# A chunked state-space scan followed by hash-routed experts on one Trainium2 core: scan scalings and routing arithmetic on GpSimd, halved masked copies, and other orders of gathers, weight sums and products

## The chip, the cores and the metric

The kernel runs on one core of a Trainium2 chip. The metric is the device time of one execution in microseconds (us). Lower is better. TensorE, VectorE, ScalarE and GpSimd have instruction queues of their own, in the profile PE, DVE, ACT and POOL; SyncE (SP) issues most transfers, ScalarE some, and GpSimd all the indirect ones (gathers and scatters by a list of row numbers).

## The reference

Two computations follow each other. The first is a scan over 768 tokens for 4 batches of 8 heads (head width 32, state width 16), in chunks: within a chunk a causal product, across chunks a state that decays.

```python
cum = np.cumsum(la, axis=-1)                      # la = log(clip(a)), per chunk
L = np.exp(cum[:, :, :, None] - cum[:, :, None, :]) * causal
M = np.einsum('bhin,bhjn->bhij', Cc, Bc) * L
y[:, :, sl] = np.einsum('bhij,bhjd->bhid', M, xc) \
            + np.einsum('bhin,bhnd->bhid', Cc, state) * np.exp(cum)[:, :, :, None]
state = decay_full * state + sum_over_j(Bc * decay_from_j * xc)
```

The second takes the 3072 rows of 256 numbers that come out, sends each to one of 8 experts by its token's id, and applies that expert's two layers (256 to 1024 to 256, all float32):

```python
expert_idx = token_ids * np.int64(2654435761) % np.int64(E)
for e in range(E):
    mask = expert_idx == e
    out[mask] = np.maximum(x[mask] @ w1[e], 0.0) @ w2[e]
```

## The kernel before, in words

The order on each engine is the order of the code: nothing reorders it. Each engine works its queue off in order, so an instruction that waits holds all those behind it on that engine.

**The scan** works in six pieces of 128 tokens of all four batches (`k` = 0 to 5), with time units of 64. B and C are loaded in four larger pieces of 1, 1, 2 and 2 (`PIECES`, `load_rows`). `factors` gives each row its decay factors, `scale_rows` multiplies the loaded rows by them (512 or 1024 columns, always on VectorE, L234), `turn_rows` transposes them in 32 by 32 blocks (VectorE, L241), and `mask_c` makes two copies of C with every other head zero (ScalarE). `gram(k)` is the product of B and C, 64 small products into four PSUM banks (L523). `masked(k)` copies its lower triangle into a block whose other half stays zero (`copy_predicated`, 2048 columns, L528), `intra(k)` multiplies that with x (L572), `dstates(k)` and `states(k)` make the states (L551, L555 on VectorE), and `inter(k)` adds C times the state (L583). `y_evict` and `y_store` bring the piece to DRAM. In the loop (L664 to L693) piece k's `states`, then some work of `piece(k)`, `intra` and `inter` come first, then `gram`, `masked` and `dstates` of piece k + 1.

**The routing** is spread over `piece(k)` and the loop's end: the experts' ids as a mask (`rt_ids`, `rt_mask`, L289 to L302), counts (`rt_count`), places, halves and overflow of each expert (`rt_prefix`, `rt_place`, L316 to L359, in piece 2), the slot of each token (`rt_rank`, L366 to L369, on GpSimd; `rt_slot_a` to `rt_slot_d`, L373 to L400, in piece 3), one-hot rows (`rt_lanes`: twelve on GpSimd, L411, and twelve on VectorE, L407; `rt_tiles`), products that turn them into a table (`rt_table`) and the index lists (`to_index`, L432 to L453). The first five gathers (`gather`, L480) follow.

**The experts** (place 0 is the one with the most tokens) do both layers with seven products instead of eight per 2 by 2 block (Strassen's scheme in Winograd's form). So there are sums on weights (`sums_w1`, L711 to L714; `sums_w2`, L720 to L723), on tokens (`sums_x`) and on hidden rows (`sums_h`), all on VectorE. `step(p)` runs expert p's first layer (`up`, L770) beside expert p - 1's second (`down`, L812), in seven slots: sums, two `up` products, a tile of gathered tokens turned for the next expert (`turn_x`, L488), a finished tile turned and scattered (`put`, L838 to L847), one `down`. The four sums of `sums_w1` stand in slot 0, the four of `sums_w2` in slot 1, and `ask(1)` asks for one more gather in every slot from the third on. A gather needs one of eight buffers (`gpool`), a scatter one of four (`o_sb`). Steps 0 to 7 are followed by step 8, which has only the last second layer; then four tiles are put out (L948 to L950). A loop over overflow tiles (L958) runs as often as a count says, here not at all.

The chain of small sums before a product's result:

```python
        elif what == 7:                                    # up(), L787
            dve.tensor_tensor(out=u3, in0=src, in1=st["p1"], op=OP.add)
            z = ps[:, st["z"], 0:2 * n].rearrange("q (i n) -> q i n", i=2)
            dve.tensor_tensor(out=hq(2), in0=z, in1=u3, op=OP.add)
            act.activation(hq(2), hq(2), AF.Relu)
```

## Time and profile before

| what | value |
|---|---|
| time, median of three runs | 287.68 us (284.52 to 287.95) |
| the profiled execution | 285.23 us |
| its span | 283.4 us |
| TensorE busy | 224.9 us (79%), 2577 products |
| weight loads on TensorE | 205.7 us (73%) |
| VectorE busy | 201.5 us (71%) |
| ScalarE busy | 76.3 us (27%) |
| GpSimd busy | 79.0 us (28%) |
| mean granted TensorE clock | 0.92 of full speed |

The span is one execution seen by the hardware profiler. Busy shares are means over stages: to 86 us the scan, from there to about 270 the experts, then the end. Products on TensorE are pipelined and their ends modelled, so a busy TensorE is not one at its peak. "[0.9 <-DVE x L1]" behind a row says how long the engine was idle before it and which instruction ended that; "issue" is idle time for which the profile shows no wait. A granted clock of 1.0 is 2.4 GHz, 0.5 is 1.2 GHz.

### The profile page before, as it was taken

To read this page: it belongs to the slowest core of one execution; us is meant where nothing else is said; L and a number is where in the kernel's file an instruction comes from. 1 tells how busy PE (TensorE), PEld (TensorE's weight loads), DVE (VectorE), ACT (ScalarE), POOL (GpSimd) and SP (SyncE) were. 2 spreads that over 40 slices of the span, in tenths; PEclk is the share of its full clock that TensorE was granted. 3 is DMA by queue.
4 is the path that set the end of the run, shared out by engine and by line. 5 is a ranking of instruction groups with operands and counts; after the bars stand their busy time and mean duration, and the time that the engine had idled before them with its cause. 6 is when DMAs were issued, how large, how long until landed. Compare 5 with 4: busy or idle time off the path is not lost. (4 is left out here: it accounts for less than half of the span.)

```text
span 283.4 us, 6377 instructions
## 1 busy us (share of the span) xinstructions
PE 224.9 (79%) x2577; PEld 205.7 (73%) x2579; DVE 201.5 (71%) x393; ACT 76.3 (27%) x177; POOL 79.0 (28%) x113
## 2 busy tenths in 40 slices
PE   7885775576579768798799989499989999999820
PEld 2773654465469758788689989399979999998810
DVE  7879768999808529977977958836876886776310
ACT  4314152043116512210312223221242242313010
POOL 8800003019443760001121501710132130312250
PEclk9689799579958997999999999989999999999995
DMA  5899998507958334015316305610901500500110
GB/s 127 135 173 141 173 178 176 192 22 207 294 173 245 97 106 148 19 21 191 123 57 208 126 2 185 203 38 5 312 20 58 166 26 13 172 33 6 51 59 1
DMA packets 51890, 33.19 MB, mean 117 GB/s; under 512 B 30714, under 2 KB 46194, under 8 KB 51860
## 3 DMA queue, kind: packets, MB, share of 16 engines
q1 hardware_dynamic: 47444, 24.41, 34.4%
q0 software_dynamic: 2400, 6.43, 7.0%
q10 hardware_dynamic: 2016, 1.93, 2.3%
q8 instruction: 21, 0.34, 0.6%
q14 instruction: 9, 0.07, 0.1%
HBM read 26.47 MB, written 6.42 MB: 116 GB/s over the span
## 5 line engine op out<-in xcount | busy, mean ns | idle before, releaser
L847 POOL DMA_INDIRECT out_dram<-o_sb,idx_out x25 | 27.9, 1117 | 73.7 <-ACT o_sb L843 58.9
L480 POOL DMA_INDIRECT xg<-y_tokens,idx_in x25 | 27.5, 1098 | 75.3 <-PE ps L838 46.6
L770 PE MATMUL ps<-t,s 128*128 128x202 f32 (+7 forms) x192 | 37.6, 333 | 2.2 <-DVE t L730 1.6
L770 PEld LDWEIGHTS ps<-t,s 128*128 128x128 f32 x192 | 32.8, 194 | 3.2 <-ACT xT L494 1.8
L812 PE MATMUL ps<-t,s 128*128 128x202 f32 (+7 forms) x192 | 34.9, 326 | 0.0
L812 PEld LDWEIGHTS ps<-t,s 128*128 128x128 f32 x192 | 31.3, 190 | 0.0
L770 PE MATMUL ps<-xT,w 128*128 128x202 f32 (+7 forms) x128 | 26.2, 342 | 0.0
L792 ACT ACTIVATE hx<-hx 128x404 f32<-128x404 f32 (+7 forms) x16 | 8.4, 525 | 57.6 <-DVE hx L791 57.6
L770 PEld LDWEIGHTS ps<-xT,w 128*128 128x128 f32 x128 | 22.6, 200 | 0.8 <-ACT p1e L777 0.7
L572 PE MATMUL ps<-x,w 128*64 128x64 f32 x384 | 15.6, 251 | 7.1 <-issue 2.6
L572 PEld LDWEIGHTS ps<-x,w 128*64 128x64 f32 x384 | 14.7, 164 | 8.3 <-issue 4.5
L770 PE MATMUL ps<-t,w 128*128 128x202 f32 (+7 forms) x64 | 14.5, 351 | 7.1 <-DVE u L789 5.6
L528 DVE COPY_PREDICATED w<-cmask,ps 128x2048 f32<-128x2048 int32 x6 | 15.2, 2532 | 4.9 <-PE ps L523 4.9
L770 PEld LDWEIGHTS ps<-t,w 128*128 128x128 f32 x64 | 11.0, 198 | 9.1 <-DVE u L789 7.3
L838 PE MATMUL ps<-ident,xT 128*128 128x128 f32 x50 | 9.8, 281 | 6.7 <-ACT o_sb L843 6.1
L812 PE MATMUL ps<-hx,s 128*128 128x202 f32 (+7 forms) x64 | 12.1, 331 | 2.5 <-DVE xT L830 2.5
L770 PE MATMUL ps<-xT,s 128*128 128x202 f32 (+7 forms) x64 | 13.8, 344 | 0.0
L843 ACT ACTIVATE o_sb<-ps 128x256 f32<-128x256 f32 x23 | 8.7, 380 | 18.6 <-PE ps L838 12.2
L411 POOL TENSOR_SCALAR laneoh<-iota,lane 128x128 bf16<-128x128 f32 x12 | 9.0, 765 | 16.6 <-DVE stile L400 16.6
L494 ACT ACTIVATE xT<-ps 128x256 f32<-128x256 f32 x23 | 8.6, 377 | 16.6 <-PE ps L488 14.7
L523 PE MATMUL ps<-ce,bt 32*64 32x128 f32 x384 | 8.9, 315 | 5.1 <-ACT ce L251 2.8
L812 PEld LDWEIGHTS ps<-hx,s 128*128 128x128 f32 x64 | 10.5, 189 | 3.4 <-DVE xT L830 3.4
(189 smaller groups left out, 442.1 us busy)
## 6 DMA issues: line engine op xcount, KB each, us to landing
w<-in_moe_w_dram SPq DMA_DIRECT2D x8, 1024.0 KB, 6.4
w<-in_moe_w_dram SPq DMA_DIRECT2D x13, 512.0 KB, 4.8
x<-in_x_dram SPq DMA_DIRECT2D x12, 256.0 KB, 6.4
y_tokens<-y_sb SPq DMA_DIRECT2D x6, 512.0 KB, 3.4
w<-in_moe_w_dram ACTq DMA_DIRECT2D x3, 512.0 KB
raw<-in_B_dram SPq DMA_DIRECT2D x8, 128.0 KB, 6.0
raw<-in_C_dram SPq DMA_DIRECT2D x8, 128.0 KB, 4.7
raw<-in_B_dram SPq DMA_DIRECT2D x8, 64.0 KB, 2.1
```

Source lines behind the costliest of these rows:

```text
L411: eng.tensor_scalar(out=laneoh[:, i], in0=iota_n, scalar1=lane[:, i:i + 1], scalar2=None, op0=OP.is_equal)
L480: pool_e.indirect_dma_start(out=xg[k], out_offset=None, in_=y_dram[0:n, :], in_offset=bass.IndirectOffsetOnAxis(ap=idx_in[:, k:k + 1], axi ...
L494: act.activation(o, i, AF.Copy)
L523: pe.matmul(out=ps[u * T:(u + 1) * T, BM + b, g * P:(g + 1) * P].rearrange("q (e i) -> q e i", e=2), lhsT=bts[k][r, g, c], rhs=ces[k][r, g ...
L528: dve.copy_predicated(out=m_sb, mask=cmask.bitcast(I32).rearrange("q j i -> q (j i)").unsqueeze(1).to_broadcast([P, NB, 2 * G * T]), data= ...
L572: pe.matmul(out=o[:, 0], lhsT=m_sb[:, b, h * T:(h + 1) * T], rhs=xs[k][:, b * H + h], start=first, stop=True, skip_group_check=True)
L770: pe.matmul(out=ps[:, bank, i * n:(i + 1) * n], lhsT=lhs[:, (q0 + i) * P:(q0 + i + 1) * P], rhs=rhs, start=(first and i == 0), stop=True, ...
L792: act.activation(hq(2), hq(2), AF.Relu)
L812: pe.matmul(out=ps[:, bank, 0:n], lhsT=lhs(q), rhs=rhs(q), start=(first and q == 0), stop=True, skip_group_check=True)
L838: pe.transpose(out=ps[:, bank, i * P:(i + 1) * P], in_=xT[:, i, k * P:(k + 1) * P], identity=ident)
L843: act.activation(o_sb, ps[:, bank, 0:DM], AF.Copy)
L847: st = pool_e.indirect_dma_start(out=out[:], out_offset=bass.IndirectOffsetOnAxis(ap=idx, axis=0), in_=o_sb, in_offset=None, bounds_check= ...
```

## The change

In the scan, five of the eight scalings (`scale_rows` for C of piece 1 and for all of load pieces 2 and 3) go to GpSimd, as do the small sums for the unit decays (`rg`), the mask of the ids, and the routing's arithmetic on shifts, overflow and slots, partly with other operations of the same value (a comparison is a subtraction and a test of the sign). `gram`, `masked` and `intra` work in two halves of two batches each, so that the products of a half can begin when its half of the masked copy is done. The ids are turned before the loop, the loads are issued in another order (ids and x of piece 0 ahead of piece 1's rows), GpSimd clears the last two x buffers after its first scaling, and the table's products stand ahead of piece 5's `gram`. The eight decays by head go to ScalarE.

In the experts, a gather is asked for whenever a tile has been turned, the sums on weights are dealt out one to a slot (`sums_w2` from the fourth slot on), the `up` products of steps 1 and 2 and the `down` products of all steps have another order, and the last expert's second half begins at a multiple of 128 slots. The last `down` is done in two column parts of 128 and 56, each put out at once, after the two tiles that are complete before; a drain stands on GpSimd behind the tiles of the expert before it.

```diff
+        if pj == order[-1]:
+            at = -(-at // P) * P
...
     load_rows(0, 0, sp4)
     load_rows(0, 1, [act] * NB)
+    sp_e.dma_start(out=tok, in_=tok_h.bitcast(I32).rearrange("(c p two) -> c p two", c=NCH, two=2))
+    load_x(0)
     load_rows(1, 0, sp4)
     load_rows(1, 1, sp4)
-    load_x(0)
-    load_x(1)
-    sp_e.dma_start(out=tok, in_=tok_h.bitcast(I32).rearrange("(c p two) -> c p two", c=NCH, two=2))
...
+    def rt_shift():
+        pool_e.tensor_tensor(out=ovt, in0=tend, in1=ovt, op=OP.subtract)
...
+    def rt_slots():
         g2 = small("g2", sh)
+        eng = pool_e
+        for g, from_, far in ((g1, half, sel[:, 2]), (g2, half2, ovt)):
+            eng.tensor_tensor(out=g, in0=val, in1=ex(from_), op=OP.subtract)
+            eng.tensor_scalar(out=g, in0=g, scalar1=0.0, scalar2=None, op0=OP.is_ge)
+            eng.tensor_tensor(out=g, in0=g, in1=ex(far), op=OP.mult)
...
+    def masked(k, bs):
+        b0, b1 = bs[0], bs[-1] + 1
         dve.copy_predicated(
+            out=m_sb[:, b0:b1],
+            mask=cmask.bitcast(I32).rearrange("q j i -> q (j i)").unsqueeze(1).to_broadcast([P, len(bs), 2 * G * T]),
+            data=ps[:, BM + b0:BM + b1])
+
+    LO, HI = range(0, NB // 2), range(NB // 2, NB)
...
     def piece(k):
         if k == 0:
-            scale_rows(dve, 2, 0)
             turn_rows(2, 0)
         elif k == 1:
-            scale_rows(dve, 2, 1)
             turn_rows(2, 1)
             mask_c(2, (act, act))
+            state["who"] = rt_prefix()
+            scale_rows(pool_e, 3, 0)
+        elif k == 2:
+            rt_place(state["who"])
+            rt_shift()
+            load_regs()
+            turn_rows(3, 0)
             mask_c(3, (act, act))
-            rt_mask()
-        elif k == 2:
-            state["n"], state["poh"] = rt_prefix()
-            rt_place(state["n"], state["poh"])
-            load_regs()
-            scale_rows(dve, 3, 0)
-            turn_rows(3, 0)
-            rt_rank(pool_e)
+            scale_rows(pool_e, 3, 1)
+            rt_slots()
         elif k == 3:
-            scale_rows(dve, 3, 1)
             turn_rows(3, 1)
             mask_c(4, (act, act))
...
+        if k == 4:
+            rt_table(BB, 0)
         if k + 1 < NPR:
-            gram(k + 1)
-            masked(k + 1)
+            gram(k + 1, LO)
+            masked(k + 1, LO)
+            gram(k + 1, HI)
+            masked(k + 1, HI)
             dstates(k + 1)
...
+    UPS = [(0, 6, 1), (0, 5, 2), (0, 7, 1), (2, 6, 0), (0, 4, 1), (0, 3, 2), (2, 7, 0), (2, 5, 2), (2, 4, 0), (2, 3, 2)]
+    DOWN = [1, 2, 6, 7, 5, 4, 3]
...
                 turn_x(k)
                 turned.add(k)
+                ask(1)
...
             if s == 0 and 0 < p < E - 1:
-                sums_w1(p + 1, dve)
-            if s == 1 and 0 < p < E:
-                sums_w2(p, dve)
-            if s >= 2:
-                ask(1)
+                sums.append(sums_w1(p + 1))
+            if s == 3 and p > 0:
+                sums.append(sums_w2(p))
+            for x in sums:
+                next(x, None)
...
+    for s, w in enumerate([1, 2, 6, 7, 4, 5]):
+        if s < 4:
+            sums_h(E - 1, s)
+        down(E - 1, w, 3 + BK[w], dst)
+        if puts:
+            put(puts.pop(0), BQ)
+            if not puts:
+                pool_e.drain()
+    assert not puts
+    mid = [k for k in outs if done_at[k] == E - 1 and k * P < base[E - 1, 1]]
+    for i, k in enumerate(mid):
+        put(k, (BQ, BT)[i % 2], (act, dve)[i % 2])
+    down(E - 1, 3, 3 + BK[3], dst, PARTS)
```

What this does to the queues, at three places. First GpSimd from its tables to the routing; x_99 and x_100 are the last two x buffers. Before:

```order
L176 IOTA iota_165 128x8
L176 IOTA iota_167 128x8
L176 IOTA iota_169 128x128
L176 IOTA iota_171 128x24
L176 IOTA iota_173 128x1
L188 MEMSET ctab 128x1 x24
L192 MEMSET x_99 64x32x32 x2
L192 MEMSET x_100 64x32x32 x2
L366 TENSOR_TENSOR val<-pin,cnt 128x192
L367 TENSOR_TENSOR val<-val,cnt 128x192
L368 TENSOR_SCALAR val<-val 128x192
L369 TENSOR_TENSOR val<-val,shift 128x8x8
```

and now, from the mask on, where `rows` are scaled rows:

```order
L314 TENSOR_SCALAR mask_266<-eid 128x24 x8
L240 TENSOR_TENSOR rows_397<-raw_119,fac_244 128x512
L625 MEMSET x_99 64x32x32 x2
L625 MEMSET x_100 64x32x32 x2
L240 TENSOR_TENSOR rows_489<-raw_475,fac_310 128x1024
L240 TENSOR_TENSOR rows_491<-raw_482,fac_310 128x1024
L347 TENSOR_TENSOR shift<-sel,pin 128x8
L348 TENSOR_SCALAR shift<-shift 128x8
L349 TENSOR_SCALAR half_289<-sel 128x8
L350 TENSOR_TENSOR ov<-pin,shift 128x8
L351 TENSOR_TENSOR ov<-ov,half_289 128x8
L353 TENSOR_TENSOR who<-poh,iota_190 128x64
```

Three scalings and the mask stand there now, the clearing of the x buffers lies behind the first of them, and the routing's small steps follow.

Second, GpSimd from its one-hot rows (laneoh) to the last scatter; xg is a gathered tile, out_dram the output. Before:

```order
L411 TENSOR_SCALAR laneoh<-iota_169,lane 128x128 x12
L480 DMA xg<-y_tokens,idx_in 128x256 x23
L847 DMA out_dram<-o_sb,idx_out 3072x256
L480 DMA xg<-y_tokens,idx_in 128x256 x2
L847 DMA out_dram<-o_sb,idx_out 3072x256 x24
```

and now:

```order
L412 TENSOR_SCALAR laneoh<-iota_194,lanes 128x128 x12
L481 DMA xg<-y_tokens,idx_in 128x256 x19
L863 DMA out_dram<-o_sb,idx_out 3072x256
L481 DMA xg<-y_tokens,idx_in 128x256 x3
L863 DMA out_dram<-o_sb,idx_out 3072x256
L481 DMA xg<-y_tokens,idx_in 128x256
L863 DMA out_dram<-o_sb,idx_out 3072x256
L481 DMA xg<-y_tokens,idx_in 128x256
L863 DMA out_dram<-o_sb,idx_out 3072x256 x2
L481 DMA xg<-y_tokens,idx_in 128x256
L863 DMA out_dram<-o_sb,idx_out 3072x256 x20
```

Before, 23 gathers stood ahead of the first scatter; now 19 do, and the last six gathers alternate with scatters.

Third, VectorE in piece 3, from the scaling of C's last rows to the slots' sum (slot_f). Before:

```order
L234 TENSOR_TENSOR rows_970<-raw_480,fac_334 128x1024
L241 STREAM_TRANSPOSE ct<-rows_970 128x4x8x32
L373 TENSOR_TENSOR g_268<-val,sel 128x192
L374 TENSOR_TENSOR g_268<-g_268,sel 128x192
L376 TENSOR_SCALAR half_982<-sel 128x8
L381 TENSOR_TENSOR g_984<-val,half_982 128x192
L382 TENSOR_TENSOR g_984<-g_984,ovt 128x192
L383 TENSOR_TENSOR val<-val,sel 128x192
L384 TENSOR_TENSOR g_268<-g_268,g_984 128x192
L387 TENSOR_TENSOR val<-val,g_268 128x192
L388 TENSOR_TENSOR val<-val,mask_264 128x192
L393 TENSOR_REDUCE slot_f<-val 128x24
```

and now, from the masked copy before it to the one behind it (lanes is the same sum):

```order
L524 COPY_PREDICATED w_131<-cmask,ps 128x1024 x2
L550 TENSOR_TENSOR zd<-d_sb,z 128x256
L554 TENSOR_TENSOR z<-zd,ge_sb 128x256
L550 TENSOR_TENSOR zd<-d_sb,z 128x256
L554 TENSOR_TENSOR z<-zd,ge_sb 128x256
L247 STREAM_TRANSPOSE ct<-rows_837 128x4x8x32
L395 TENSOR_REDUCE lanes<-val 128x24
L396 CAST slot_i<-lanes 128x24
L398 TENSOR_SCALAR part<-slot_i 128x24
L399 TENSOR_SCALAR part<-slot_i 128x24
L401 CAST lanes<-part 128x48
L524 COPY_PREDICATED w_131<-cmask,ps 128x1024 x2
```

The scaling and eight slot instructions are gone from VectorE, and the slots' sum, ahead of the masked copy, reads what GpSimd writes.

## Rows read from the trace of the kernel before

**Rows 1.** Stretches (us): busy time and instructions per engine, PEclk, DMA share, GB/s

```profile
core 0: us, PE busy (x) PEld busy (x) DVE busy (x) ACT busy (x) POOL busy (x), PEclk, DMA share, GB/s
...
110.13:131.42 21.29, 18.18 (x100) 17.22 (x100) 17.45 (x32) 3.50 (x8) 1.02 (x1) 0.96 0.29 96
131.42:152.18 20.76, 17.86 (x106) 16.86 (x106) 16.84 (x31) 4.12 (x10) 3.94 (x3) 1.00 0.37 119
152.18:173.51 21.33, 20.58 (x128) 19.77 (x127) 16.56 (x31) 6.43 (x17) 4.81 (x4) 1.00 0.26 82
173.51:198.85 25.34, 21.33 (x124) 20.75 (x124) 16.66 (x31) 5.95 (x15) 8.05 (x7) 0.93 0.36 118
198.85:220.47 21.62, 20.31 (x129) 19.45 (x129) 16.39 (x31) 6.74 (x18) 5.20 (x5) 1.00 0.36 125
220.47:239.98 19.51, 19.51 (x126) 18.91 (x125) 16.20 (x31) 5.94 (x16) 3.38 (x3) 1.00 0.24 75
```

**Rows 2.** Order of time, VectorE in the scan: start us, us, engine, line, operation

```profile
25.61 2.52 DVE L528 COPY_PREDICATED w<-cmask,ps 128x2048 f32<-128x2048 int32 x1
...
30.92 1.22 DVE L234 TENSOR_TENSOR rows<-raw,fac 128x1024 f32<-128x1024 f32 x1
...
32.17 2.02 DVE L241 STREAM_TRANSPOSE ct<-rows 128x1024 f32<-128x1024 f32 x1
...
36.91 2.52 DVE L528 COPY_PREDICATED w<-cmask,ps 128x2048 f32<-128x2048 int32 x1 [2.54 <-PE ps L523]
...
41.78 0.55 DVE L316 TENSOR_TENSOR_SCAN pin<-rstc,cnt 128x192 f32<-128x192 f32 x1
...
48.09 0.17 DVE L359 TENSOR_TENSOR ovt<-ovt,sel 128x8 f32<-128x8 f32 x1
...
51.40 2.53 DVE L528 COPY_PREDICATED w<-cmask,ps 128x2048 f32<-128x2048 int32 x1
...
58.68 0.34 DVE L373 TENSOR_TENSOR g<-val,sel 128x192 f32<-128x192 f32 x1
...
61.24 0.36 DVE L388 TENSOR_TENSOR val<-val,mask 128x192 f32<-128x192 f32 x1
...
62.88 2.53 DVE L528 COPY_PREDICATED w<-cmask,ps 128x2048 f32<-128x2048 int32 x1
...
75.20 0.17 DVE L435 TENSOR_SCALAR idx_in<-tva 128x25 int32<-128x25 f32 x1
```

**Rows 3.** Order of time in the scan, SyncE's x loads and GpSimd

```profile
7.79 6.27 SPq L124 DMA_DIRECT2D x<-in_x_dram  x4
...
9.54 4.12 POOL L192 MEMSET x<- 64x1024 f32 x4
...
42.49 0.59 POOL L366 TENSOR_TENSOR val<-pin,cnt 128x192 f32<-128x192 f32 x1 [28.83 <-DVE pin L316]
...
46.05 0.29 POOL L369 TENSOR_TENSOR val<-val,shift 128x64 f32<-128x64 f32 x1 [1.44 <-DVE shift L345]
```

**Rows 4.** Single lines: count, duration in ns (min/median/max), first and last start

```profile
L411 POOL TENSOR_SCALAR laneoh<-iota,lane x12: 592/610/1403, 63.0 to 71.4; 128x128 bf16<-128x128 f32 x12
...
L555 DVE TENSOR_TENSOR z<-zd,ge_sb x10: 424/425/544, 22.1 to 77.6; 128x256 f32<-128x256 f32 x10
```

**Rows 5.** TensorE's waits from 28 to 86 us: total us, times, longest

```profile
PE ps L572 <- issue: 2.6, 1, 2.6
```

**Rows 6.** Order of time in the experts: a scatter, ScalarE's and TensorE's wait

```profile
158.90 1.37 POOL L847 DMA_INDIRECT out_dram<-o_sb,idx_out  x1 [0.30 <-issue]
...
181.78 0.38 ACT L843 ACTIVATE o_sb<-ps 128x256 f32<-128x256 f32 x1 [6.18 <-DMA out_dram<-o_sb,idx_out]
...
182.22 0.44 PE L838 MATMUL ps<-ident,xT 128*128 128x128 f32 x2 [4.01 <-ACT o_sb L843]
```

**Rows 7.** The end: GpSimd's last scatter, and the closing line's drains (ns)

```profile
275.40 0.98 POOL L847 DMA_INDIRECT out_dram<-o_sb,idx_out  x1 [0.30 <-issue]
...
L1030 POOLq DRAIN  x3: 45/103/4155, 278.4 to 283.2; - x3
```

More of the change, by code (lines that the diff above doesn't have):

```diff
@@ L312 @@
     dve.memset(rstc[:, :, 0:1], 0.0)
+    ones_e = route.tile([P, E], F32)
+    dve.memset(ones_e, 1.0)
+    half = sel[:, 0]
+    nn = pin[:, :, NCH - 1]
     def rt_prefix():
@@ L398, in rt_slot_d @@
                           op0=OP.logical_shift_right)
-        dve.tensor_copy(out=lane, in_=part[:, 0])
-        dve.tensor_copy(out=stile, in_=part[:, 1])
+        dve.tensor_copy(out=lanes, in_=part)
     CG = 6
@@ L514, in decays_by_heads, with gram @@
         for e in range(2):
-            dve.tensor_scalar(out=ge_sb[:, :, :, e], in0=g_sb, scalar1=par[:, e:e + 1], scalar2=None, op0=OP.mult)
-    def gram(k):
+            act.activation(ge_sb[:, :, :, e], g_sb, AF.Copy, scale=par[:, e:e + 1])
+    def gram(k, bs):
         for g in range(G):
             for u in range(2):
-                for b in range(NB):
+                for b in bs:
                     r = slice(32 * b, 32 * b + 32)
@@ L568, in intra @@
     def intra(k):
-        for h in range(H):
-            for b in range(NB):
-                o, first = y_out(b, h, 1)
-                pe.matmul(out=o[:, 0], lhsT=m_sb[:, b, h * T:(h + 1) * T], rhs=xs[k][:, b * H + h],
-                          start=first, stop=True, skip_group_check=True)
+        for bs in (LO, HI):
+            for h in range(H):
+                for b in bs:
+                    o, first = y_out(b, h, 1)
+                    pe.matmul(out=o[:, 0], lhsT=m_sb[:, b, h * T:(h + 1) * T], rhs=xs[k][:, b * H + h],
+                              start=first, stop=True, skip_group_check=True)
     def inter(k):
@@ L799, in up, with down @@
             act.activation(hq(1), hq(1), AF.Relu)
-    def down(p, what, bank, st):
+        if what in (5, 7) and "z" in st and "u3" in st:
+            dve.tensor_tensor(out=hq(2), in0=st["z"], in1=st["u3"], op=OP.add)
+            act.activation(hq(2), hq(2), AF.Relu)
+    def down(p, what, bank, st, parts=()):
         n = HALF[p]
@@ L810, in down @@
         first = what in (1, 6, 5)
+        if parts:
+            for i, (c0, c1) in enumerate(parts):
+                for q in range(Q4):
+                    pe.matmul(out=ps[:, bank, c0:c1], lhsT=lhs(q), rhs=rhs(q)[:, c0:c1], start=False, stop=True,
+                              skip_group_check=True)
+                dve.tensor_tensor(out=xT[:, 0, slots(p, 1)][:, c0:c1], in0=ps[:, bank, c0:c1], in1=st["u2"][:, c0:c1],
+                                  op=OP.add)
+                put(slots(p, 1).start // P + i, (BQ, BT)[i], (act, dve)[i], c1 - c0)
+            return
         for q in range(Q4):
@@ L902, in step @@
             else:
-                ups = [(q0, w, BK[w]) for q0 in (0, 2) for w in (UP_E if p < NEAR - 1 else UP)]
+                ups = UPS if p < NEAR - 1 else [(q0, w, BK[w]) for q0 in (0, 2) for w in UP]
+        ups = list(ups)
+        sums = []
         downs = list(DOWN) if p > 0 else []
@@ L944, in step @@
             load_w2(p + 1)
-    for p in range(E + 1):
+    for p in range(E):
         step(p)
-    last = [k for k in outs if done_at[k] == E - 1]
-    for i, k in enumerate(last):
-        put(k, (BQ, BT, 0, 1)[i % 4], (act, dve)[i % 2])
+    dst = {}
+    puts = [k for k in outs if done_at[k] == E - 2]
+    for s, w in enumerate([1, 2, 6, 7, 4, 5]):
[11 more added lines that the diff above has]
+    down(E - 1, 3, 3 + BK[3], dst, PARTS)
     _, rn = nc.values_load_multi_w_load_instructions(
```

242 lines of the change are left out of this document (113 added, 129 removed).

## The prediction

> **What bounds the kernel now.** I read the table of stretches first, then the order of time inside the scan and inside the experts, then who waits for whom, then the end. A piece is 128 tokens of each of the four batches; the scan has six, k = 0 to 5, and the experts run in nine steps, 0 to 8. Four things are to be seen.
>
> The scan's loop hangs on VectorE's own order. Per piece it runs the state sums, a scaling (1.22 us), a transposition (2.02) and the masked copy (2.52 for 2048 columns), and TensorE's products of the piece start only when the whole masked copy is over [rows 2]. Between the masked copies of pieces 2 and 3 stands the whole routing, 41.78 to 48.26 us; between those of 3 and 4 stand nine slot instructions, 58.68 to 61.60 [rows 2]. The copies of pieces 1 to 4 end at 28.1, 39.4, 53.9 and 65.4 [rows 2].
>
> The expert steps take 19.5 us where nothing is in the way: step 6, TensorE busy all the time [rows 1]. Steps 1 and 2 take 21.3 and 20.8 with TensorE busy 18.2 and 17.9, step 3 21.3 with 20.6, step 4 25.3, step 5 21.6 with 20.3 [rows 1].
>
> Step 4's excess is one stall: ScalarE waits 6.18 us for an earlier scatter's buffer, TensorE 4.01 us for ScalarE [rows 6]. The first scatter started at 158.90, right behind a gather, since GpSimd's queue held all but two of the gathers ahead of it [rows 6]. The step's granted clock is 0.93, and TensorE's busy time is 1.8 us above step 6's [rows 1].
>
> At the end four scatters follow one another on GpSimd after the last product, 0.98 us each and 0.30 between, the last from 275.40 on, and a drain of 4.16 us on GpSimd's queue closes the program [rows 7].
>
> **The scan, part by part.** The sum is made against the profiled execution: 285.2 us, 283.4 of them span; the median of the three runs is 287.7, the lowest 284.5.
>
> *Scalings on GpSimd.* Five of eight move there. The trace has none on that engine. A product of two inputs took 0.59 us for 192 columns and 0.29 for 64 [rows 3], so 2.3 ns a column and 0.15 fixed: 1.3 us for 512 columns, 2.5 for 1024. The lower end is the 1.22 that VectorE takes; upward I allow twice the value, 5.0, because the scaling reads three strides at once and the rows don't. I take 2.5.
>
> *Start.* Half copies let piece 0's products begin when half is copied, and the small sums of decays leave VectorE. But GpSimd first clears two x buffers (4.12 us [rows 3]), now behind the scaling of piece 1, and only then scales for piece 2. VectorE's order puts that transposition ahead of piece 1's masked copy, so it now waits for GpSimd. The loads of piece 1's rows are issued behind the ids and two x loads, which at 1.6 us an issue [rows 3] puts their landing, an estimate, at 13 to 14; 13.7 + 1.3 + 4.1 + 2.5 = 21.6, say 22, where VectorE could come at 20. Masked copy 1 then ends at 22 + 2.0 + 2.5 = 26.5: 1.5 gained.
>
> *Pieces 1 to 2.* The scaling (1.2) and the mask leave; the first seven routing instructions come in (about 2.7 of the 6.5, an estimate by their share), but they lie in VectorE's idle time of 2.54 before masked copy 2 [rows 2]; the product on the ids that held TensorE is made before the loop. Copy 2 ends near 36: 2 more gained.
>
> *Pieces 2 to 3.* Of 6.5 us of routing seven instructions stay, like the last at 0.17 or little more [rows 2], 1.3; 2.7 have moved forward, the rest is GpSimd's. The scaling goes: 14.5 - 5.2 - 1.2 = 8.1 between the ends of the copies. ScalarE's load of the experts' numbers now stands ahead of the mask of this piece's C, which I charge with 0.5. Copy 3 ends near 44.5: 9.4 gained in all.
>
> *Pieces 3 to 4.* Scaling and eight slot instructions leave VectorE (4.1). In their place GpSimd does the scaling (2.5) and ten slot instructions of 0.59 and more [rows 3], 6.6 with their waits, after the scaling before and the shift: from about 41 to 51. VectorE is ready for the slots' sum at 48 and waits 3. Masked copy 4 is queued behind that sum. It ends at 55, against 65.4: 10.2 gained.
>
> *Piece 4 to the gathers.* The table's products now stand ahead of piece 5's on TensorE and wait for GpSimd's twelve one-hot rows; VectorE's masked copy 5 follows, and the index only then. The token index, written at 75.20 [rows 2], comes near 66.4: 8.8 gained. The first gathers follow as before.
>
> *What comes to light.* TensorE has gaps that the profile calls issue, up to 2.6 us [rows 5], at places where VectorE was mostly the later one. With VectorE faster I charge 2. Scan: **-6.8**.
>
> One rule speaks against all this. VectorE's two-input sums and GpSimd's reading instructions did meet: the one-hot row on GpSimd took 0.61 in the middle and 1.40 at most, the state product 0.43 in the middle and 0.54 at most [rows 4]. The Trainium skill, SBUF — State Buffer, section "Who interferes with whom", says that a VectorE instruction with two SBUF inputs and a GpSimd instruction that reads SBUF exclude each other, the second one blocked until the first has finished. GpSimd's 1.40 agrees with it in size, VectorE's 0.54 does not: it was delayed by 0.1, not by a whole row of 0.6. So I leave the states at their price; the other reading is a rival below.
>
> **The experts.** Steps 1 and 2: the products come in an order where none reads what VectorE has just been handed, and the sums on weights are dealt out one per slot instead of four in a row. VectorE's 17 us and TensorE's 18 remain, so I put the steps at 18.5 and 18.3: 5.3 gained (at least 2, if VectorE's lag stays; at most 6). Step 3 falls to its busy 20.6 (0.7) and step 5 to its 20.3 (1.3), as the sums no longer come in lumps of four. Step 4: a gather is asked for when a buffer is freed, so the scatters stand between the gathers and none waits for buffers of later tiles; 4.0 of stall and 1.5 of slow clock go, 5.5. Sum 12.8; for a new wait somewhere I take 0.8 off: **-12** (bounds -8 and -14).
>
> **The end.** The last product is done in two column parts of 128 and 56, each followed by its own scatter, and two of the four tiles go out before it. GpSimd's scatters stay 1.28 apart, so the chain begins at about 269 and its last starts near 273: **-2.5**. A drain on GpSimd is added after step 6's tiles are out, where GpSimd has some 4 us to spare. What the closing drain then takes no row shows: 0.05 us where nothing was issued before it, 4.16 after fifty indirect transfers [rows 7]. Four stand behind the new one, so I go by the row nearer to that: 0.5, **-3.6**; at the other end 0.
>
> 285.2 - 6.8 - 12 - 2.5 - 3.6 = 260.3; with half the distance to the median of the runs, 261.5.
>
> **The rivals.** *GpSimd becomes the scan's bound.* At 5.0 us a scaling, three of the four long ones stand on the path: 7.5 more, the scan gains nothing, 268 to 269. For it: the wait at piece 3 is there already at 2.5. Against: by rows 3 a product costs 0.15 us and 2.3 ns a column, not 5.
>
> *VectorE is blocked.* If each of four groups of state sums waits for a running scaling to end, up to 2.5 each, the scan loses 10 and ends 3 behind: 271. That is the page's rule taken in full. Against it stands the 0.54 of rows 4.
>
> *The stall of step 4 stays*, because the new scatter order still meets slow transfers: 5.5 less, 267.
>
> *Nearly no change:* both of the first two with the experts' lower bound: 285.2 + 3 + 3 - 8 - 2.5 = 280.7.
>
> *Slower:* the same chain on GpSimd, if scalings with three strides cost over 10 us each. Four scalings at 7.5 more are 30, which uses up the gain of 25 and ends near 290. It decides from 9 us on. Nothing in rows 3 comes near.
>
> **How the numbers follow.** Forecast 0.62, GpSimd as the bound 0.17, blocked VectorE 0.06, the stall stays 0.06, nearly no change 0.06, slower 0.03. A measurement of this kernel tells 2% (5.8 us) from no change. Faster by more than that: 0.62 + 0.17 + 0.06 + 0.06 = 0.91; within it 0.06; slower 0.03. The range starts at the best of all terms, 285.2 - 11 - 14 - 7 = 253 (the scan's 11 with scalings as short as VectorE's), with 2 for the runs' spread below, 251, and ends where the two middle rivals with the runs' spread (2.4) end, 274.
>
> **What would show it.** Right: masked copies ending near 26, 36, 44 and 55; VectorE idle for about 3 us before the slots' sum, with GpSimd named; steps 1 and 2 near 18.5 and step 4 near 20; no wait of ScalarE for a scatter; a closing drain under 1 us. Wrong: scalings on GpSimd far from 2.5, transpositions that wait for GpSimd in every piece, the first gather later than 70, or a closing drain still at 4.

## The result, and the profile after

| | before | after |
|---|---|---|
| median of four runs | 286.10 us (282.06 to 287.95) | 257.75 us (257.01 to 258.11) |
| ratio, 95% interval | | 0.9087 [0.9024, 0.9149] |
| profiled execution, its span | 285.23, 283.4 | 257.79, 256.1 |
| TensorE, VectorE, GpSimd busy | 79%, 71%, 28% | 87%, 74%, 38% |

Medians here and below are over all runs of a kernel, ratios over its fast runs alone; the profiled executions of scan_only, experts_only and no_drain lie 1.5 to 1.9% above their kernels' fastest run. By the medians 28.4 us were gained; the forecast's sum was 24.9. The page of after, busy time by engine, the clock in 40 slices, and the chain that ended last:

```profile
PE 223.3 (87%) x2584; PEld 206.1 (80%) x2584; DVE 188.9 (74%) x362; ACT 77.2 (30%) x180; POOL 97.6 (38%) x152
...
PEclk9658997698595799999999999999999999999995
...
PE 58%; DVE 14%; DMA 12%; issue 6%; POOL 4%; ACT 3%; ACTq 0%; POOLq 0%
```

From the 15th slice to the last but one the granted clock stands at nine tenths or more: from step 1 to step 6 TensorE no longer stops. The stretches of steps 1 to 6, each from a step's first product to that of the next, answer to [rows 1]:

```profile
core 0: us, PE busy (x) PEld busy (x) DVE busy (x) ACT busy (x) POOL busy (x), PEclk, DMA share, GB/s
103.53:120.58 17.05, 17.02 (x98) 16.53 (x99) 16.26 (x32) 4.22 (x9) 1.00 (x1) 1.00 0.40 131
120.58:137.72 17.14, 17.14 (x105) 16.89 (x105) 16.04 (x32) 3.99 (x10) 4.93 (x4) 1.00 0.49 152
137.72:158.08 20.36, 20.28 (x127) 19.89 (x127) 16.73 (x32) 6.42 (x17) 8.49 (x7) 1.00 0.32 105
158.08:177.67 19.59, 19.48 (x124) 19.13 (x124) 16.10 (x31) 5.87 (x15) 3.57 (x3) 1.00 0.39 126
177.67:197.74 20.07, 19.95 (x130) 19.56 (x130) 16.00 (x31) 6.76 (x18) 5.23 (x5) 1.00 0.46 152
197.74:217.19 19.45, 19.32 (x126) 18.98 (x126) 15.92 (x31) 6.07 (x16) 3.27 (x3) 1.00 0.22 73
```

TensorE is busy for all but 0.1 us of each step. Steps 1 and 2 went from 21.29 and 20.76 to 17.05 and 17.14, step 4 from 25.34 to 19.59.

The order of time in the scan, GpSimd first, then VectorE; this answers to [rows 2]:

```profile
19.78 1.93 POOL L240 TENSOR_TENSOR rows<-raw,fac 128x1024 f32<-128x1024 f32 x1
...
35.60 1.94 POOL L240 TENSOR_TENSOR rows<-raw,fac 128x1024 f32<-128x1024 f32 x1
...
48.96 0.62 POOL L391 TENSOR_TENSOR val<-val,mask 128x192 f32<-128x192 f32 x1
```

```profile
20.66 1.33 DVE L554 TENSOR_TENSOR z<-d_sb,ge_sb 128x256 f32<-128x256 f32 x1 [1.22 <-ACT d_sb L540]
...
22.48 0.43 DVE L554 TENSOR_TENSOR z<-zd,ge_sb 128x256 f32<-128x256 f32 x1
...
25.21 2.59 DVE L524 COPY_PREDICATED w<-cmask,ps 128x1024 f32<-128x1024 int32 x2 [0.32 <-PE ps L518]
...
34.00 2.60 DVE L524 COPY_PREDICATED w<-cmask,ps 128x1024 f32<-128x1024 int32 x2 [0.49 <-PE ps L518]
36.49 1.32 DVE L550 TENSOR_TENSOR zd<-d_sb,z 128x256 f32<-128x256 f32 x1
...
44.52 2.58 DVE L524 COPY_PREDICATED w<-cmask,ps 128x1024 f32<-128x1024 int32 x2 [2.30 <-PE ps L518]
...
50.23 2.03 DVE L247 STREAM_TRANSPOSE ct<-rows 128x1024 f32<-128x1024 f32 x1
52.11 0.54 DVE L395 TENSOR_REDUCE lanes<-val 128x24 f32<-128x192 f32 x1
...
54.91 2.60 DVE L524 COPY_PREDICATED w<-cmask,ps 128x1024 f32<-128x1024 int32 x2 [1.53 <-PE ps L518]
```

and TensorE's products of B and C for pieces 3 and 4:

```profile
42.47 2.92 PE L518 MATMUL ps<-ce,bt 32*64 32x128 f32 x64 [3.32 <-ACT ce L257]
...
53.74 1.62 PE L518 MATMUL ps<-ce,bt 32*64 32x128 f32 x64 [1.99 <-ACT ce L257]
```

A scaling of 1024 columns takes GpSimd 1.93 us. The masked copies of pieces 1 to 4 end at 27.8, 36.6, 47.1 and 57.5; 26.5, 36, 44.5 and 55 had been forecast. The slots' sum at 52.11 follows right behind the transposition: GpSimd's last slot instruction had ended at 49.58, so VectorE doesn't wait for it. It waits for TensorE instead, 2.30 before the copy at 44.52, and TensorE's 64 products of piece 3 took 2.92 us at a granted clock of 0.50, those of piece 4 1.62 at 1.00. And a VectorE sum that takes 0.43 otherwise takes 1.33 and 1.32 where a scaling runs on GpSimd.

What TensorE waits for up to the first product of the experts (total us, times, longest), and the order of time around its last early gather:

```profile
PE ps L518 <- ACT ce L257: 7.7, 3, 3.3
PE ps L489 <- DMA xg<-y_tokens,idx_in: 6.9, 4, 4.3
PE ps L426 <- DVE tab L421: 3.1, 2, 2.6
```

```profile
69.28 0.17 DVE L436 TENSOR_SCALAR idx_in<-tva 128x25 int32<-128x25 f32 x1
...
75.46 1.00 POOL L481 DMA_INDIRECT xg<-y_tokens,idx_in  x1 [0.31 <-issue]
...
75.89 0.38 SPq L473 DMA_DIRECT2D w<-in_moe_w_dram  x1
...
82.25 0.29 PEld L489 LDWEIGHTS ps<-ident,xg 128*128 128x128 f32 x2 [4.69 <-issue]
82.28 0.66 PE L489 MATMUL ps<-ident,xg 128*128 128x128 f32 x2 [4.32 <-DMA xg<-y_tokens,idx_in]
```

The index is written at 69.28, 5.9 earlier than before (75.20 in [rows 2]). But the fifth early gather, issued at 75.46, is waited for until 82.28, while 1 MB of weights issued at 75.89 moves. TensorE stands still for 4.3 us and then starts at half clock, as the next two stretches show (the clock is the third number from the right):

```profile
78.00:82.30 4.30, 0.01 (x1) 0.05 (x1) 4.22 (x8) 0.00 (x0) 2.71 (x3) 0.50 1.01 299
82.30:86.50 4.20, 4.20 (x14) 4.18 (x15) 3.73 (x7) 1.40 (x3) 3.28 (x4) 0.50 0.32 101
```

At the end, the added drain and the drains of the closing line, which answer to [rows 7] (ns, least, middle, most):

```profile
L984 POOLq DRAIN  x1: 5253/5253/5253, 240.9 to 240.9; - x1
```

```profile
L1069 POOLq DRAIN  x3: 46/103/387, 254.9 to 255.8; - x3
```

### The profile page after: what moved, and what is told of

It reads as the page before. It is cut to its first block, busy times and chain, and to the rows that moved or that the text cites. A ratio compares the mean times of both kernels' runs of the same rounds, so it can differ in the third digit from the quotient of the medians.

```text
span 256.1 us, 6422 instructions
## 1 busy us (share of the span) xinstructions
PE 223.3 (87%) x2584; PEld 206.1 (80%) x2584; DVE 188.9 (74%) x362; ACT 77.2 (30%) x180; POOL 97.6 (38%) x152
## 3 DMA queue, kind: packets, MB, share of 16 engines
q10 hardware_dynamic: 2016, 1.93, 2.7%
## 4 chain that ended last, share of the span: by engine, by line
PE 58%; DVE 14%; DMA 12%; issue 6%; POOL 4%; ACT 3%; ACTq 0%; POOLq 0%
PE ps L774 25%; PE ps L825 20%; DMA out_dram<-o_sb,idx_out 10%; PE ps L518 3%; POOL laneoh L412 3%; DMA xg<-y_tokens,idx_in 3%; PE ps L489 2%; DVE w L524 2%; DVE ct L247 2%; PE ps L537 2%; DVE u L793 1%; DVE zd L550 1%; PE ps L854 1%; ACT ce L257 1%; PE ps L225 1%
## 5 line engine op out<-in xcount | busy, mean ns | idle before, releaser
L863 POOL DMA_INDIRECT out_dram<-o_sb,idx_out x25 | 28.4, 1138 | 71.3 <-ACT o_sb L859 57.1
L481 POOL DMA_INDIRECT xg<-y_tokens,idx_in x25 | 26.5, 1061 | 63.4 <-PE ps L854 35.2
L774 PE MATMUL ps<-xT,w 128*128 128x202 f32 (+7 forms) x128 | 26.5, 346 | 0.0
L803 ACT ACTIVATE hx<-hx 128x404 f32<-128x404 f32 (+7 forms) x16 | 8.4, 525 | 52.4 <-DVE hx L802 52.4
L524 DVE COPY_PREDICATED w<-cmask,ps 128x1024 f32<-128x1024 int32 x12 | 15.4, 1348 | 8.8 <-PE ps L518 7.3
L717 DVE TENSOR_TENSOR s<-w 128x512 f32<-128x512 f32 x32 | 21.8, 681 | 0.0
L518 PE MATMUL ps<-ce,bt 32*64 32x128 f32 x384 | 13.7, 348 | 7.7 <-ACT ce L257 7.7
L518 PEld LDWEIGHTS ps<-ce,bt 32*64 32x64 f32 x384 | 11.7, 175 | 8.5 <-ACT ce L257 8.1
L489 PE MATMUL ps<-ident,xg 128*128 128x128 f32 x50 | 10.0, 289 | 6.9 <-DMA xg<-y_tokens,idx_in 6.9
L572 PEld LDWEIGHTS ps<-x,w 128*64 128x64 f32 x384 | 12.7, 146 | 2.4 <-issue 2.1
L572 PE MATMUL ps<-x,w 128*64 128x64 f32 x384 | 13.7, 232 | 0.7 <-issue 0.7
L495 ACT ACTIVATE xT<-ps 128x256 f32<-128x256 f32 x23 | 8.5, 376 | 18.2 <-PE ps L489 18.2
L489 PEld LDWEIGHTS ps<-ident,xg 128*128 128x128 f32 x50 | 6.7, 146 | 8.4 <-issue 4.7
L800 ACT ACTIVATE hx<-hx 128x404 f32<-128x404 f32 (+7 forms) x16 | 8.3, 525 | 13.1 <-DVE hx L799 13.1
```

What stands on the lines that cost most here:

```text
L481: pool_e.indirect_dma_start(out=xg[k], out_offset=None, in_=y_dram[0:n, :], in_offset=bass.IndirectOffsetOnAxis(ap=idx_in[:, k:k + 1], axi ...
L489: pe.transpose(out=ps[:, bank, i * P:(i + 1) * P], in_=t[:, i * P:(i + 1) * P], identity=ident)
L495: act.activation(o, i, AF.Copy)
L518: pe.matmul(out=ps[u * T:(u + 1) * T, BM + b, g * P:(g + 1) * P].rearrange("q (e i) -> q e i", e=2), lhsT=bts[k][r, g, c], rhs=ces[k][r, g ...
L524: dve.copy_predicated(out=m_sb[:, b0:b1], mask=cmask.bitcast(I32).rearrange("q j i -> q (j i)").unsqueeze(1).to_broadcast([P, len(bs), 2 * ...
L572: pe.matmul(out=o[:, 0], lhsT=m_sb[:, b, h * T:(h + 1) * T], rhs=xs[k][:, b * H + h], start=first, stop=True, skip_group_check=True)
```

## The experiments

A time alone tells the kernels apart poorly, because the scan's end moves by a few us from kernel to kernel where the scan is the same (the index between 69.2 and 71.1 in eight traces). The order of time on TensorE is sharper: with the new order of the experts a step's length repeats to 0.02 us from kernel to kernel. So the table has, for each profiled execution, when the index is written, when the first product of the experts and step 1 begin, and how long steps 1 to 5 take (from the first product of a step to that of the next), and beside them the times of all runs. A ratio is to runs of before on the same chip. Step 0, from its own first product to that of step 1, takes 8.2 us, but 12.2 in before, 11.7 in sums_lump, 11.8 in w2_second_late and 9.9 in scale_dve: there TensorE stops in it for up to 2.5 us that the profile puts down to issue, and the start of step 1 holds these 1.7 to 4.0 us as well.

| kernel | index | first product | step 1 begins | steps 1 to 5 | median us | ratio to before |
|---|---|---|---|---|---|---|
| before | 75.20 | 86.39 | 110.13 | 21.3, 20.8, 21.3, 25.3, 21.6 | 286.10 | |
| after | 69.28 | 82.74 | 103.53 | 17.05, 17.14, 20.36, 19.58, 20.07 | 257.75 | 0.9087 |
| scan_only | 70.88 | 84.88 | 105.89 | 22.77, 20.75, 21.33, 25.80, 21.77 | 282.40 | 0.9892 [0.983, 0.9955] |
| experts_only | 76.95 | 88.74 | 109.61 | 17.05, 17.14, 20.36, 19.58, 20.07 | 260.91 | 0.9144 [0.9044, 0.9243] |
| no_drain | 70.18 | 84.25 | 104.75 | as after | 261.47 | 0.9112 [0.8979, 0.9246] |
| before_drain | 75.00 | 87.19 | 108.67 | 22.77, 20.75, 21.34, 24.36, 22.02 | 281.91 | 0.9800 [0.9713, 0.9888] |
| ask_old | 70.51 | 84.42 | 105.68 | 17.05, 17.14, 20.36, **24.46**, 20.08 | 264.89 | 0.9205 [0.9124, 0.9285] |
| ups_old | 69.39 | 83.22 | 103.89 | **18.10, 18.27**, 20.36, 19.58, 20.07 | 260.97 | 0.9097 [0.9024, 0.9171] |
| sums_lump | 69.24 | 80.16 | 103.87 | **19.39, 18.91, 21.19, 20.21, 21.26** | 265.48 | 0.9277 [0.9225, 0.9329] |
| scale_dve | 73.21 | 84.42 | 106.44 | as after | 260.70 | 0.9121 [0.9069, 0.9173] |
| w2_late | 70.82 | 84.53 | 105.23 | as after | 259.77 | 0.9051 [0.8983, 0.9118] |
| w2_second_late | 71.05 | 82.22 | 106.04 | 16.65, then as after | 259.57 | 0.9033 [0.8965, 0.9101] |
| table_late | 67.74 | 81.82 | 102.80 | as after | 256.92 | 0.8923 [0.8830, 0.9017] |
| table_and_w2 | 68.07 | **78.34** | **99.34** | as after | **253.41** | 0.8860 [0.8809, 0.8910] |

**The two halves, scan_only and experts_only.** The code up to the release of the scan's buffers is taken from one kernel, all behind it from the other:

```diff
-    (scan of before)  a_ctx.close()  (experts of before)
+    (scan of after)   a_ctx.close()  (experts of before)      # scan_only
+    (scan of before)  a_ctx.close()  (experts of after)       # experts_only, with the new line on slots
```

> The changed scan with the experts and the end as they were before. The forecast's term for the scan is 6.8 us, so by it 286.1 - 6.8 = 279.3 us (0.976 of before). A rival from the trace of after: there the first product of the experts starts only 3.7 us earlier than before (82.74 against 86.39), because TensorE waits 4.3 us for a gather; if the rest of the scan's gain was made good only by the new order of the experts, this kernel gains 3.7 and comes to 282.4.

> The scan as before with the changed experts and end (and the last expert's second half starting on a tile of its own, as in after). By the forecast's terms 12 + 2.5 + 3.6 = 18.1 us are gained: 268.0 us (0.937 of before). By the rival named for the scan alone, everything after the first product of the experts belongs to this half: 28.4 - 3.7 = 24.7 gained, 261.4 us (0.914).

The scan alone brings 3.1 us (1.1%, between 1.3 and 4.9: under 2%, but the interval leaves out 0), the experts with the end 24.5 (8.6%, between 21.7 and 27.4). Together that is 27.6, near the 26.1 that after's ratio gives: the halves add up. The forecast's split of 6.8 and 18.1 falls, the split read from the first product of the experts (3.7 and 24.7) holds in both runs.

**The drain, no_drain and before_drain.** no_drain takes the drain out of after, before_drain puts one into before, ahead of the last four scatters:

```diff
-            if not puts:
-                pool_e.drain()
```

```diff
         step(p)
+    pool_e.drain()
     last = [k for k in outs if done_at[k] == E - 1]
```

> The changed kernel without the drain on GpSimd after step 6's tiles. If the closing drain costs by the indirect transfers issued since the last drain, it is back at about 4.2 us in the profile, the time is 257.8 + 3.8 = 261.5 us. If it was short because the transfers now end earlier, it stays near 0.4 us and the time at 257.8.

> The kernel before with one drain on GpSimd ahead of the last four scatters, where GpSimd idles for 7.1 us. By the count of transfers: closing drain near 0.4 us, 286.1 - 3.8 = 282.3 us (0.987 of before). If the closing drain's 4.16 us came from the last scatters' own landing, it stays and the time is 286.1 or, with the added drain on the path, up to 4 more.

The closing line of no_drain, then of before_drain, whose added drain stands first:

```profile
L1067 POOLq DRAIN  x3: 40/103/4163, 255.4 to 260.1; - x3
```

```profile
L948 POOLq DRAIN  x1: 5045/5045/5045, 262.7 to 262.7; - x1
```

```profile
L1031 POOLq DRAIN  x3: 51/103/387, 277.9 to 278.8; - x3
```

The closing drain is 4.16 us where all fifty indirect transfers stand before it, and 0.387 where a drain stood four scatters earlier, in either kernel. So it isn't the last scatters' landing. The cost moves to the earlier drain, which takes 5.0 to 5.3 us, and lies in GpSimd's idle time there: 7.12 us in before_drain, 4.70 in after. In after that is a little short. From place 6's last product to the end of the last scatter it takes 16.30 us, without the drain 15.66. So the drain nets 3.8 - 0.6 = 3.1 in after; the 3.7 between the two times holds a scan that ended 1.2 later as well. These are readings of traces: the ratios of no_drain and after overlap, and before_drain's 2.0% (1.1 to 2.9) is more than the 1.3% that 3.8 us are.

**The order of gathers, ask_old.**

```diff
                 turned.add(k)
-                ask(1)
...
+            if s >= 2:
+                ask(1)
```

> The changed kernel with the gathers asked for as before, one a slot from slot 2 on, instead of one for each buffer freed. By the forecast's step the stall of step 4 is a matter of GpSimd's order: it comes back with 4.0 us and 1.5 of slow clock, 263.3 us. Rival: the stall came from TensorE's and VectorE's lag in steps 1 to 3, which the other edits removed; the time stays at 257.8.

Of the steps, step 4 alone grows, by 4.9 us; another 2.2 of the 7.1 us between the two times lie ahead of step 1, which begins that much later. The order of time in step 4, a stretch that after does not have, and the step as a whole:

```profile
163.49 1.61 POOL L863 DMA_INDIRECT out_dram<-o_sb,idx_out  x1 [0.30 <-issue]
...
165.41 1.00 POOL L863 DMA_INDIRECT out_dram<-o_sb,idx_out  x1 [0.30 <-issue]
...
166.71 1.50 POOL L863 DMA_INDIRECT out_dram<-o_sb,idx_out  x1 [0.30 <-issue]
...
167.71 0.38 ACT L859 ACTIVATE o_sb<-ps 128x256 f32<-128x256 f32 x1 [5.38 <-DMA out_dram<-o_sb,idx_out]
...
168.15 0.69 PE L854 MATMUL ps<-ident,xT 128*128 128x128 f32 x2 [3.22 <-ACT o_sb L859]
```

```profile
160.24:184.70 24.46, 21.14 (x123) 20.55 (x123) 16.11 (x31) 5.98 (x15) 8.07 (x7) 0.93 0.36 124
```

The three scatters come in one row behind a gather, ScalarE waits 5.38 us for one of them, TensorE 3.22 for ScalarE, and the step's clock is 0.93 as in [rows 1]. It is the stall of [rows 6], and GpSimd's old order brings it back with all else as in after.

**The products' order and the weight sums, ups_old and sums_lump.**

```diff
-                ups = UPS if p < NEAR - 1 else [(q0, w, BK[w]) for q0 in (0, 2) for w in UP]
+                ups = [(q0, w, BK[w]) for q0 in (0, 2) for w in (UP_E if p < NEAR - 1 else UP)]
```

```diff
-                sums.append(sums_w1(p + 1))
-            if s == 3 and p > 0:
-                sums.append(sums_w2(p))
-            for x in sums:
-                next(x, None)
+                list(sums_w1(p + 1))
+            if s == 1 and p > 0:
+                list(sums_w2(p))
```

> The changed kernel with the upper products of steps 1 and 2 in their order before; the sums on weights stay dealt out. Steps 1 and 2 are 5.7 and 3.6 us shorter in after (17.05 and 17.14) than in the other traces with the old experts (22.77 and 20.75). If the products' order made that, some 7 to 9 us come back: 265 to 267. If the lumps of four sums made it, under 2 come back: at most 259.8.

> The changed kernel with the sums on weights in two lumps of four again, behind slots 0 and 1. The old order of products gave back only 2.2 us of the 9.3 by which steps 1 and 2 differ. If the lumps made the rest, step 1 grows by 3 to 4.6 us, step 2 by 1.4 to 2.5, step 3 by 1 and step 5 by 1 to 2, and the time comes to 265 to 268 us. If the lumps are hidden once the products' order is new, the steps stay within 0.5 and the time at 258.

The old order of products gives back 1.05 and 1.13 us in steps 1 and 2. The lumps give back 2.34 and 1.77 there, and 0.83, 0.63 and 1.19 in steps 3 to 5. Steps 1 and 2 of sums_lump, and under them those of scan_only, which has both old:

```profile
103.87:123.26 19.39, 17.11 (x99) 16.46 (x99) 17.18 (x32) 3.46 (x8) 1.00 (x1) 1.00 0.35 115
123.26:142.17 18.91, 17.41 (x105) 16.87 (x105) 16.55 (x31) 3.91 (x10) 4.66 (x4) 1.00 0.40 124
```

```profile
105.89:128.66 22.77, 19.17 (x99) 18.20 (x100) 18.15 (x33) 4.22 (x9) 1.00 (x1) 0.93 0.29 98
128.66:149.41 20.75, 17.86 (x106) 16.85 (x105) 16.83 (x31) 4.13 (x10) 3.93 (x3) 1.00 0.39 120
```

Step 1 of scan_only is 5.7 longer than in after, with the order alone 1.1 and with the lumps alone 2.3; step 2 is 3.6 longer, and 1.1 and 1.8. That leaves 2.3 and 0.7 us for which neither edit accounts. They can't be put down to the two together, for scan_only has a third thing old that bears on these steps: the order of the `down` products, in which product 3 needs the bank that product 5 holds until the sum behind product 7. In before, from 110 to 220 us, TensorE waits so:

```profile
PE ps L770 <- DVE u L789: 3.7, 2, 1.9
PE ps L812 <- DVE xT L830: 1.7, 2, 0.9
```

The second is that sum, once in step 1 and once in step 2, and scan_only has the same two waits of 0.9; after, ups_old and sums_lump have none. What is left of step 1 is busy time, 19.17 us against 17.02, at a granted clock of 0.93 where either edit alone keeps 1.00. No run took the order of `down` back by itself, or the two edits together, so how these last 2.3 and 0.7 us divide stays open. Neither edit alone made the 9.3 us: ups_old's 261.0 us lies between its two forecasts, and sums_lump came to the 265 to 268 that was expected of it, with step 1 growing by 2.3 instead of 3 to 4.6.

**The scalings, scale_dve.** The four scalings of 1024 columns go back to VectorE, each ahead of its transposition:

```diff
-    scale_rows(pool_e, 2, 0)
-    scale_rows(pool_e, 2, 1)
...
         if k == 0:
+            scale_rows(dve, 2, 0)
             turn_rows(2, 0)
```

> The changed kernel with the four scalings of the last two load pieces back on VectorE, each right ahead of its transposition. If VectorE's order is the bound of the scan, as the forecast had it, four scalings of 1.22 us come onto the path, less the two stalls of 0.9 us that VectorE has in after beside GpSimd's scalings: 3.1 more, 260.9 us, and idx_in near 72.4. If ScalarE's masks of C and TensorE at half clock bind the scan now, VectorE has the room: idx_in within 1 us of 69.3 to 70.9, the time near 258.

The index comes at 73.21, 2.2 to 4.0 us later than in the eight traces whose scan is that of after, so VectorE's order does bind the scan up to there. What of it reaches the time isn't shown: 260.7 us is 3.0 more than after, but the ratios overlap (0.9121 and 0.9087), and 1.7 of this run's later step 1 are the stops of TensorE in step 0.

**The gathers, w2_late, w2_second_late, table_late and table_and_w2.**

First w2_late, which issues the load by ScalarE (`act`) behind the early turns, then w2_second_late, then table_late; table_and_w2 has the last two edits together.

```diff
-            load_w2(0)
...
+    load_w2(0, act)
```

```diff
-    load_w2(1)
+    load_w2(1, act)
```

```diff
-        if k == 4:
-            rt_table(BB, 0)
...
             masked(k + 1, HI)
+            if k == 4:
+                rt_table(BB, 0)
```

> The changed kernel with the second layer's first weights (1 MB) issued by ScalarE behind its last early turn, so after the last early gather has landed, instead of by SyncE right behind the gathers. In after the last early gather took 6.7 us from issue to the product that reads it, and TensorE waited 4.3 us. Theory: the megabyte crowds the gather out; without it the wait falls to about 1, the first product comes near 79.5 and the time falls by 3, to 254.8 us. Rival: the gather is held by the half megabyte of w1 issued at 69.55 or by the rows themselves; the wait stays, 257.8, or the late weights hold VectorE's sums and it is slower by up to 2.

> The changed kernel with the table's products moved behind piece 5's products of B and C on TensorE; VectorE's order stays. In after the table waits 2.6 us for VectorE and holds those products, which then run at half clock, and the masked copy and the index follow: idx_in at 69.28. Theory: TensorE's order held VectorE; idx_in comes near 66.8 and the time falls by 2.5, to 255.3 us. Rival: the first product of the experts is set by the landing of the last gather among weight transfers, not by the index: the wait for gathers grows by as much and the time stays at 257.8.

> The changed kernel with the second expert's w2 (1 MB) issued by ScalarE behind its last early turn, instead of by SyncE behind the last store of y. It is this transfer that starts at 75.89 in after, behind the issue of the last early gather (75.46); the first expert's w2, which the run w2_late moved, had been issued at 63.39. Theory: from 77 to 79 this megabyte fills the DMA engines and holds the gather; behind it the gather lands in about the 3 us of the others, the wait of 4.3 falls under 1, the first product comes near 79.5 and the time falls by 3, to 254.8 us. Rival: the half megabyte of w1 from 69.55 is what delays the gathers; the first product stays near 82.7 to 84.5 and the time at 257.8.

> Both edits of the runs table_late and w2_second_late together: the table's products behind piece 5's products of B and C, and the second expert's w2 issued by ScalarE behind its last early turn. table_late brought the index to 67.74 and the first product to 81.82, with a gather waited for 4.5 us; w2_second_late had no such wait, but TensorE's own products of piece 5 trickled. Theory: with the index early and no megabyte ahead of the gathers, the first product comes near 78.5 and step 1 begins 3 earlier than in after (103.5): 254.5 us. Rival: what sets step 1's start is the last store of y and the gathers of far tiles behind it, which neither edit brings forward enough; step 1 begins at 103 to 106 as in every run with the changed scan, and the time is 257 to 259.5.

w2_late moved the wrong megabyte: the one at 75.89 is the second expert's. Nothing improved, and it says nothing on the theory. table_late brings the index to 67.74 and the first product to 81.82, not 2.5 but 0.9 earlier, as TensorE then waits 4.5 us for the same gather; its time is 0.8 us below after's by the medians, and its ratio lower by more (0.8923 against 0.9087, the intervals just apart), so how much it gains stays open. w2_second_late has no wait for gathers, but for another reason as well: TensorE itself came late. Its order of time, products of piece 5:

```profile
75.17 0.35 PE L583 MATMUL ps<-z,ct 32*64 32x64 f32 x5 [0.38 <-issue]
75.94 0.34 PE L583 MATMUL ps<-z,ct 32*64 32x64 f32 x5 [0.41 <-issue]
76.69 0.35 PE L583 MATMUL ps<-z,ct 32*64 32x64 f32 x5 [0.41 <-issue]
```

Groups of five products with 0.4 us between them, seven times: so this run leaves the theory open. Nor have sums_lump and scale_dve, whose w2 was not moved, a wait for an early gather: stops of the same kind held TensorE, the last store of y and the weights back there (the weights to 80.11 and 84.52). Both edits together settle it. table_and_w2's order of time on TensorE:

```profile
75.44 1.04 PE L489 MATMUL ps<-ident,xg 128*128 128x128 f32 x4 [0.49 <-DMA xg<-y_tokens,idx_in]
77.40 1.15 PE L489 MATMUL ps<-ident,xg 128*128 128x128 f32 x4 [0.93 <-DMA xg<-y_tokens,idx_in]
78.34 0.88 PE L774 MATMUL ps<-xT,w 128*128 128x202 f32 x2
```

The wait of 4.5 us that table_late has ahead of the last early turn is gone, with the weights' issue the only difference between the two kernels. The first product comes at 78.34, step 1 at 99.34, and the time is 253.41 us (251.50 to 253.97). The intervals of its ratio and of after's don't touch: this version beats both kernels.

## Why the prediction came out right

The sum was right (257.75 against 261.5, inside the range), but two of its terms were wrong in opposite directions, the scan's by 3.7 us too much and the experts' by at least 4.1 too little. That they cancelled is luck. The runs replace the terms thus:

| term | forecast | measured | from |
|---|---|---|---|
| scan | -6.8 | -3.1 (1.3 to 4.9) | scan_only |
| steps 1 to 5 | -12 | -18.2, or -16.1 | step lengths of scan_only, or of before, against after |
| the last scatters | -2.5 | -2.2, or -1.6 with the added drain in the way | 17.86, 15.66 and 16.30 us from place 6's last product to the last scatter's end |
| closing drain | -3.6 | -3.8 for the drain itself | no_drain, before_drain |

**Scan, up to the index: nearly right.** The step "I take 2.5" for a scaling was too high: it takes 1.93. The step "VectorE is ready for the slots' sum at 48 and waits 3" did not occur: VectorE came at 52.1, GpSimd had ended at 49.6. What made VectorE late was TensorE in piece 3: it waited 3.3 us for ScalarE's mask of C, which stands behind the load of the experts' numbers (charged with 0.5), and then ran at half clock, 2.92 us for products that take 1.62 in piece 4. Its waits for the other two masks, 2.4 and 2.0, end with VectorE's own transposition, which ScalarE waits for; behind the slots' sum it waits 3.1 for the table, and piece 5's products run at half clock again. The 2 us charged for what comes to light on TensorE were too few, and slow clock was no part of them. The index came at 69.2 to 71.1 in the traces with the changed scan as it is, 66.4 was forecast; in after 5.9 us of the 8.8 were there.

**Scan, behind the index: the step that failed.** "The first gathers follow as before" was wrong. The second expert's w2 stands behind the last store of y on SyncE's queue. In before that store left at 85.33 and the weights at 86.37, when the early gathers had landed; in after TensorE is done with piece 5 ahead of the gathers, the store leaves at 74.84, and the weights move beside the last early gather. Of the 5.9 us 2.2 were lost again. That this transfer did it is shown by table_late against table_and_w2, one trace of each, and the times agree (all of table_late's runs take longer than any of table_and_w2's).

**VectorE beside GpSimd: the row was read too lightly.** The forecast took the 0.54 of [rows 4] as the whole price of a meeting. After shows 1.33 and 1.32 instead of 0.43, and both times VectorE's sum ended some 0.28 us after GpSimd's scaling did (scalings to 21.71 and 37.54, sums to 21.99 and 37.81). So the mechanism of the rival "VectorE is blocked" is there, but only two of the five scalings met a sum, 0.9 us each, where the rival had four at up to 2.5. The Trainium skill, SBUF — State Buffer, section "Who interferes with whom", has a VectorE instruction with two SBUF inputs contend with a GpSimd instruction that reads SBUF, and whichever starts second waits. The forecast left that to a rival; these two sums agree with it, both second and both over only after the scaling. The masked copy at 25.21, which ran beside the scaling from 25.79 on, took 2.59, as long as the one at 44.52 (2.58), which met no scaling.

**Experts: the mechanism right, the size wrong.** "VectorE's 17 us and TensorE's 18 remain, so I put the steps at 18.5 and 18.3" took TensorE's busy time in before as a floor. It was none: with the same products the busy time of step 2 went from 17.86 to 17.14, and VectorE's fell too. With no gap a product's record lasts 0.33 us and the next begins after 0.17. At a gap the record before it shows its whole 0.33 and the one behind it 0.44, so each of the three gaps of step 2 leaves about 0.26 in the busy time (an estimate from these records); 0.72 went. And that step 1 ran at a granted clock of 0.93 to 0.96 with the old order was not counted as a loss. Steps 3 and 5 came to 20.36 and 20.07, as forecast (20.6 and 20.3). Step 4's 5.5 was right: it fell by 5.8, and 4.9 came back in ask_old. Against before's own steps the -12 was 4.1 short, and the 16.1 lies beyond its bound of 14: 2.6 of the 4.1 are in steps 1 and 2, 0.8 are the allowance for a new wait, which did not come in the steps.

One reading of before was distorted: its step 0 took 12.15 us where the other two traces with the old experts (scan_only, before_drain) have 8.19, and its step 1 took 21.3 where they have 22.8. The 4.0 us by which that step 0 is longer are part of the 27.3 between the two profiled spans, and no term of the forecast held them. What held TensorE's results back there at 102 to 107 us stays open.

**The end.** The drain was judged right, by the nearer row. The step "where GpSimd has some 4 us to spare" was right (4.05 in no_drain), but gave the added drain no price, and it takes 5.25. And between the last scatter's end and the closing drain every kernel with the new end has 2.6 to 3.3 us where the old end has 2.0 to 2.1; what takes that 1 us was not tried, and with it the end as a whole gained 4.4 (24.9 to 20.5 from place 6's last product), not 6.1.

Of the rivals, "the stall of step 4 stays", "GpSimd becomes the scan's bound", "nearly no change" and "slower" did not occur. "VectorE is blocked" occurred at a fifth of its price.

## What to carry to other kernels

Busy time that an engine shows in a stretch with many gaps is no floor for the stretch without them; take the floor from a stretch that runs without a gap, product by product. When a stage is made faster, list the transfers that its end sets free: here a prefetch of weights moved up by 10 us into the gathers that the next stage begins with, and cost over a third of what the stage had gained. And where two edits each lift one of two limits, try them together: the last 3.5 us of the two that lead to 253.4 came only with both. But count every difference before what is left over is called their joint gain: in steps 1 and 2 a third edit, the order of `down`, had been changed too and was never tried alone.
